# Attention steps of two batches placed at shared moments, and batch 2's landmarks summed on VectorE

## The chip, the cores and the metric

One core of one Trainium2 chip runs the whole kernel in one launch. The metric is the device time of that launch in microseconds (us), lower is better. The engines are named as in the profile: PE is TensorE's matmul stream, PEld its weight loads, DVE is VectorE, ACT ScalarE, POOL GpSimd, and SP is SyncE, whose queue issues most of the DMAs.

## What is computed

Nystrom attention over 8 batches of 8 heads (576 positions, head dimension 64, 32 landmarks), then a mixture of experts in which a token takes an expert of its own or keeps that of the token before it. Cut to what matters:

```python
q_lm = q.reshape(B, H, m, S // m, D).mean(axis=3)      # landmarks: means of 18 rows, m = 32
k_lm = k.reshape(B, H, m, S // m, D).mean(axis=3)
A, Bm, C = sm(q, k_lm), sm(q_lm, k_lm), sm(q_lm, k)    # softmax(scale * a @ b.T)
Z = Bm.transpose(0, 1, 3, 2) / (norm1(Bm) * norminf(Bm) + 1e-06)
for _ in range(6):
    Z = 2 * Z - Z @ Bm @ Z
x = A @ Z @ C @ v
...
fresh_e = int(np.argmax(logits[b, s]))
e = fresh_e if s == 0 or local_gate[b, s] < 0.5 else prev_e
out[b, s] = p[e] * (np.maximum(x[b, s] @ w1[e], 0.0) @ w2[e])
```

All inputs and outputs are float32.

## The kernel before

The tokens of a batch nearly all go to one expert, so the kernel finds that expert, `own` (L500), and runs a dense two-layer product for the batch with it; tokens of other experts are gathered at the end into slots of 128 (`slot_tokens`, `slots_end`). Batches are in a pipeline: while `expert` (L837) runs for one batch, the attention of the next is worked off in between.

**The expert.** For each of 8 batches `expert` goes over 16 steps: two passes (of 320 and of 256 rows) with 8 blocks of the hidden layer each. In a step PE does six products of the first layer (L819, into a `ph` bank), and then those of the second layer for the block before (L861 into `py` banks, L870 into `pg`). Operands are split in a high and a low part (`gh`/`gl`, `ath`/`atl`, `wh`/`wl`, `h`), which makes three products of each. These are PE's large products, on the full 128 x 128 array. For each block ACT and DVE turn the `ph` bank into `h` (L826, L831, for batch 0 also `hx` L828, L834); for each weight block ACT casts (L806) and POOL subtracts (L808).

**The attention of one batch** is a chain of small steps. `landmarks` (L190) sums 18 rows: two POOL additions of 128 x 288 (L200, into the tile `t9`) and a DVE reduction (L202), for each half of q and k. `scores_c` (L239) makes the scores of C and Bm (L251) in two groups; each group takes two of the three banks named `one`, which its exps on ACT (L262, L266) set free. `norms` (L308) is a chain of 13 small DVE instructions (L311 to L336), `newton_product` (L345) and `newton_start` (L349, L350) open the iteration, and six `newton_step` follow (PE L358, ACT L360, DVE L361). `c_transpose` (L278) and `c_v` (L297) give C @ v, `newton_w` (L365, L367), `newton_wt` (L374) and `newton_gate` (L384) give the gate's weights. `scores_a` (L398, L402), `a_max`, `a_exp`, `a_norm`, `a_back` make A. Then `gates` (L447), `fresh`, `sticky` (L481, L483, L485), `chosen` (L491 to L497), `own` (L504 to L511) choose the expert; SP reads its number and `load_w1`/`load_w2` fetch its weights. `own_rest` (L514 to L528, eight DVE instructions) and `a_split` (L434, L436) follow. `w_w1` (L774) folds the gate's weights into the first layer (PE L785, ACT L791, DVE L794).

PE runs the small products with the array cut into tiles: 32 rows by 32 columns for L345, L358, L365; 64 by 32 for L251, L384, L398, L785; 128 by 32 for L447 and most of L297. Only the transposes L278 and L374 and the sum L504 use the full array. In PE's stream a run of small products between two large ones is called a burst here.

**What sets the order.** A clock counts expert steps: batch b of the expert lasts from 16 b to 16 b + 16 (`CH` = 16). A step's `tick` calls move the clock by a quarter and emit every action that is due, `at_time(t, fn, ...)`; a `yield 0.25` inside an action puts its rest a quarter of a step later. Each engine then executes in the order of emission. `attention(b)` (L1090) gives the due times of batch b relative to t0 = (b - 1) * 16:

```python
at_time(t0 - 0.75, scores_c, st, 0)
at_time(t0 + 0.5, scores_c, st, 1)
ta, tn = [t0 + t for t in (-2.75, -1.75, -0.75, 3.25, 4, 5.5)], t0 + 2
...
for k in range(6):
    at_time(tn + 1.5 + 0.5 * k, newton_step, b, st, k)
```

So a batch's attention lies within some 14 steps, its Newton iteration within three. Batch 0's attention is `startup` (L538), ahead of all expert work, written out by hand; batch 1's whole attention lies in batch 0's expert steps, with due times of its own.

Of the kernel before, what the change touches and what calls it, by code (L numbers as in the profile page):

```python
# [23 lines left out]
P = 128  # L24
# [36 lines left out]
def nystrom_attn_then_sticky_moe(ctx, tc, qT, kT, v, wg, w12, out):  # L61
# [152 lines left out]
    def landmark_parts(st, t, a):  # L214
# [5 lines left out]
        def part(n):  # L220
# [18 lines left out]
    def scores_c(st, g, d=0.5):  # L239
# [5 lines left out]
        pc = [one.tile([P, 512]) for _ in range(2)]  # L245
# [268 lines left out]
    def own_rest(b, st):  # L514
# [4 lines left out]
                                in1=others.unsqueeze(2).broadcast_to([P, E, NBLK]), op=ALU.mult)  # L519
        pe = st["pe"]  # L520
# [17 lines left out]
    def startup(st, nx):  # L538
# [550 lines left out]
    CH = 2 * NC2  # L1089
    def attention(b):  # L1090
        st, t0 = sts[b], (b - 1) * CH
        if b > 1:
            at_time(t0 - (13 if b == 2 else 14), load, b, st)
            at_time(t0 - 11, load_v, b, st)
            for t, x, a in ((-10, "k", 0), (-9, "k", 2), (-8, "q", 0), (-7, "q", 2)):
                t = t if b > 2 else 0.75 * t
                at_time(t0 + t, landmarks, b, st, x, a)
            at_time(t0 - 0.75, scores_c, st, 0)
            at_time(t0 + 0.5, scores_c, st, 1)
            ta, tn = [t0 + t for t in (-2.75, -1.75, -0.75, 3.25, 4, 5.5)], t0 + 2  # L1100
# [3 lines left out]
        at_time(ta[0], scores_a, b, st, 0)
        at_time(ta[1], scores_a, b, st, 1)
        at_time(ta[2], a_max, b, st)
        at_time(ta[3], a_exp, st)
        at_time(ta[4], a_norm, b, st)
        at_time(ta[5], a_back, st)
        at_time(tn, norms, b, st)  # L1110
        at_time(tn + 0.5, newton_product, b, st)
        at_time(tn + 1.25, newton_start, b, st)
        for k in range(6):
            at_time(tn + 1.5 + 0.5 * k, newton_step, b, st, k)
        for k, t in enumerate((1, 1.75, 2.25)):
            at_time(tn + t, c_transpose, st, 2 * k)
        at_time(tn + 3.25, c_v, st)
        at_time(tn + 4.5, newton_w, b, st)
        at_time(tn + 5, newton_wt, b, st)
        at_time(tn + 5.5, newton_gate, b, st)  # L1120
        at_time(tn + 6.25, gates, st)
        at_time(tn + 6.5, fresh, st)
        at_time(tn + 7.25, sticky, st)
        at_time(tn + 8.25, chosen, st)
        at_time(tn + 8.75, own, b, st)
        at_time(tn + 9, get_w1, b)
        at_time(tn + 9.25, own_rest, b, st)
        at_time(tn + 9.5, a_split, b, st)
# [16 lines left out]
    at_time(3.5, lambda: w_w1(sts[0], 1))  # L1145
    at_time(7.25, own_rest, 0, sts[0])
# [67 lines left out]
```

## Time and profile before

| | |
|---|---|
| time, median of 3 runs | 523.0 us (520.9 to 524.95) |
| time of the profiled execution | 525.08 us |
| its span, first to last instruction | 523.4 us |
| PE busy | 482.6 us (92%), mean granted clock 0.962 |
| DVE, ACT, POOL busy | 325.2, 210.5, 192.6 us (62, 40, 37%) |
| DMA | 82.58 MB, mean 158 GB/s |

The page's strip of 40 slices of 13 us shows where PE is not busy and where its clock is low:

```profile
PE   6757879888999999999999999999999999889994
PEclk9759997889899999999999999999999999999998
```

A PE matmul's duration contains its passage through the array, and the next one starts before it ends. What a product costs is the distance from its start to the start of the next one. A wait is idle time of an engine, put down to what ended it.

### The profile page before, as it was taken

The page shows a single profiled execution, that of the slowest core. Times are in us where ns is not written, and L with a number is a line of the kernel's source. Part 1 is how long each engine was busy: PE and PEld are TensorE (multiplying, and loading weights), DVE is VectorE, ACT ScalarE, POOL GpSimd, SP SyncE. Part 2 cuts the span into 40 slices and gives each one's busy share as a digit, 9 for nine tenths or more (in the row PEclk, how much of TensorE's full clock was granted, in tenths as well). Part 3 has the DMA queues.
Part 4 walks back from the last instruction along what each step waited for, and adds up shares of the span by engine and source line. Part 5 has one row for each costly group of instructions (what it writes and reads, how often), then busy time and mean ns, then how long its engine had stood idle before and what let it go on. Part 6 is the DMA issues. An engine that isn't in the chain of part 4 may idle for free. (4 is left out here: it accounts for less than half of the span.)

```text
span 523.4 us, 12143 instructions
## 1 busy us (share of the span) xinstructions
PE 482.6 (92%) x4722; PEld 343.2 (66%) x4722; DVE 325.2 (62%) x957; ACT 210.5 (40%) x538; POOL 192.6 (37%) x206
## 2 busy tenths in 40 slices
PE   6757879888999999999999999999999999889994
PEld 2423557645777677757786677767775777668774
DVE  6876663847456764867476756676476736986230
ACT  2425432336224561447243722464144714341361
POOL 5212261343430562244422453166225501240653
PEclk9759997889899999999999999999999999999998
DMA  8448432284126643366317731763345111734340
GB/s 291 170 148 302 194 93 97 80 292 181 59 90 212 227 173 130 108 234 255 141 46 274 277 107 45 270 235 138 101 163 190 62 58 45 287 96 157 100 163 20
DMA packets 38621, 82.58 MB, mean 158 GB/s; under 512 B 3179, under 2 KB 4459, under 8 KB 37792
## 3 DMA queue, kind: packets, MB, share of 16 engines
q1 hardware_dynamic: 37072, 76.71, 41.4%
q0 software_dynamic: 1488, 5.07, 2.6%
q8 instruction: 38, 0.62, 0.5%
q14 instruction: 23, 0.19, 0.1%
HBM read 66.34 MB, written 15.47 MB: 156 GB/s over the span
## 5 line engine op out<-in xcount | busy, mean ns | idle before, releaser
L861 PE MATMUL py<-wh,h 128*128 128x512 f32 x528 | 175.1, 414 | 0.1
L808 POOL TENSOR_TENSOR wl<-raw,wh 128x512 fp32r<-128x512 f32 x72 | 92.0, 1285 | 149.5 <-ACT wh L806 106.9
L861 PEld LDWEIGHTS py<-wh,h 128*128 128x128 f32 x528 | 91.9, 191 | 31.6 <-issue 13.8
L831 DVE SCALAR_TENSOR_TENSOR h<-ph,h 128x256 fp32r<-128x256 f32 (+1 forms) x136 | 55.6, 409 | 86.2 <-ACT h L826 80.5
L826 ACT ACTIVATE h<-ph 128x256 fp32r<-128x256 f32 (+2 forms) x136 | 54.7, 403 | 123.0 <-PE ph L819 115.3
L861 PE MATMUL py<-wl,h 128*128 128x512 f32 x264 | 89.0, 416 | 0.0
L819 PE MATMUL ph<-ath,gh 128*128 128x320 f32 (+1 forms) x256 | 81.4, 318 | 5.6 <-DVE gl L794 1.8
L819 PE MATMUL ph<-ath,gl 128*128 128x320 f32 (+1 forms) x256 | 76.4, 298 | 0.1
L819 PE MATMUL ph<-atl,gh 128*128 128x320 f32 (+1 forms) x256 | 76.2, 298 | 0.0
L819 PEld LDWEIGHTS ph<-ath,gh 128*128 128x128 f32 x256 | 49.0, 191 | 19.7 <-issue 7.5
L861 PEld LDWEIGHTS py<-wl,h 128*128 128x128 f32 x264 | 46.0, 190 | 13.3 <-issue 3.9
L806 ACT CAST wh<-raw 128x512 fp32r<-128x512 f32 x72 | 45.1, 629 | 14.8 <-DMA raw<-w 14.8
L819 PEld LDWEIGHTS ph<-atl,gh 128*128 128x128 f32 x256 | 49.1, 192 | 2.9
L819 PEld LDWEIGHTS ph<-ath,gl 128*128 128x128 f32 x256 | 48.9, 191 | 0.4 <-DVE gl L794 0.4
L200 POOL TENSOR_TENSOR t<-k_t 128x288 f32<-128x288 f32 x24 | 17.4, 748 | 46.0 <-DVE sk L202 45.9
L361 DVE TENSOR_TENSOR et<-et,one 128x64 f32<-128x64 f32 x42 | 9.2, 220 | 35.5 <-ACT et L360 28.4
L899 POOL TENSOR_TENSOR ys<-ys,yl 64x512 f32<-64x512 f32 x8 | 10.4, 1294 | 49.0 <-ACT yl L897 49.0
L200 POOL TENSOR_TENSOR t<-q_t 128x288 f32<-128x288 f32 x24 | 17.3, 744 | 29.6 <-DVE sq L202 15.7
L360 ACT COPY et<-one 128x64 f32<-128x64 f32 x35 | 7.4, 212 | 44.0 <-PE one L358 43.0
L888 ACT ACTIVATE ys<-py,pall 128x512 f32<-128x512 f32 x32 | 20.4, 695 | 10.5 <-PE py L861 8.8
L794 DVE TENSOR_TENSOR gl<-pg,gh 128x512 fp32r<-128x512 f32 (+1 forms) x19 | 12.5, 660 | 19.1 <-ACT gh L791 19.1
L791 ACT CAST gh<-pg 128x512 fp32r<-128x512 f32 (+1 forms) x19 | 10.7, 564 | 32.5 <-PE pg L785 32.5
(313 smaller groups left out, 778.3 us busy)
## 6 DMA issues: line engine op xcount, KB each, us to landing
raw<-w SPq DMA_DIRECT2D x72, 256.0 KB, 5.5
raw<-w SPq DMA_DIRECT2D x17, 1024.0 KB, 7.1
v_t<-v SPq DMA_DIRECT2D x8, 1024.0 KB, 6.2
out<-ys SPq DMA_DIRECT2D x32, 256.0 KB, 2.2
q_t<-qT SPq DMA_DIRECT2D x6, 1152.0 KB, 5.5
k_t<-kT SPq DMA_DIRECT2D x6, 1152.0 KB, 8.2
ad<-sa POOLq DMA_DIRECT2D x8, 576.0 KB, 3.6
q_t<-qT SPq DMA_DIRECT2D x4, 576.0 KB, 9.1
```

The source lines that it names most:

```text
L200: nc.gpsimd.tensor_add(t9[:, i], src[:, a + i, :, 0:9], src[:, a + i, :, 9:18])
L361: nc.vector.tensor_add(new[:, :, 32:64], et[:, :, 32:64], pn[:, :, 32:64])
L791: nc.scalar.copy(out=gh[:, g, x], in_=ps[g])
L794: nc.vector.tensor_tensor(out=gl[:, g, x], in0=ps[g], in1=gh[:, g, x].bitcast(F32), op=ALU.subtract)
L806: nc.scalar.copy(out=wh, in_=raw)
L808: nc.gpsimd.tensor_tensor(out=wl, in0=raw, in1=wh.bitcast(F32), op=ALU.subtract)
L819: mm = nc.tensor.matmul(hp, w[:, g, c], x[:, g, s0:s0 + n], start=(i == 0), stop=(i == 5))
L826: nc.scalar.activation(out=h[:, 0:e], in_=hp[:, 0:e], func=AF.Relu)
L831: nc.vector.scalar_tensor_tensor(out=h[:, 384:384 + m], in0=hp[:, 0:m], scalar=0.0, in1=h[:, 0:m].bitcast(F32), op0=ALU.max, op1=ALU.subtract)
L861: nc.tensor.matmul(yps[k], h[:, part + i * P:part + i * P + P], w, start=(f == 0 and part == 0 and w is wh), stop=(f == NC2 - 1 and part = ...
L888: nc.scalar.mul(out=ys, in_=yp, mul=st["pw"][:, k:k + 1])
L899: nc.gpsimd.tensor_tensor(out=ys[0:64], in0=ys[0:64], in1=yl[0:64], op=ALU.add)
```

## The change

Nothing of the arithmetic changes. What changes is when, and in two places by whom, it is done:

- `attention` takes its due times from three tables: `FIRST` for batch 1, `SECOND` for batch 2, `STEADY` for the others. In `STEADY` the scores of C come 13 steps earlier (-13.75 and -11.75 rather than -0.75 and 0.5), the Newton steps lie 1.5 or 2 steps apart (0.5 before), and loads and landmarks come some 12 steps earlier. Modulo 16 the PE steps of the early part of a batch fall on the same due times as those of the late part of the batch before it, ten in all, with both `w_w1` on two of them.
- Batch 2's landmarks are reduced on DVE straight from q and k (`landmarks_alone`, eight reductions, L225), not added on POOL first.
- Batch 1's second group of C scores takes the two `py` banks.
- `own_rest` of batch 0 moves from step 7.25 into `startup`, and `own_rest` yields half a step in the middle. In `startup` the exps of a C group go ahead of the first `w_w1` on ACT, and one landmark reduction goes behind the start of the expert.
- The first casts of batch 1's second-layer weights (`cast_w2`) come 1.75 steps later, and `w_w1` of later batches a quarter earlier (`G0`).

```diff
+    def landmarks_alone(st, t, a):
+        part = landmark_parts(st, t, a)
+        part(2)
+        yield 0.25
+        s = part(2, False)
+        yield 0.5
+        landmark_scale(st, t, a, s)
...
-        pc = [one.tile([P, 512]) for _ in range(2)]
+        pc = [(bank or one).tile([P, 512]) for _ in range(2)]
...
+        yield 0.5
         pe = st["pe"]
...
+        rest = own_rest(0, st)
+        next(rest)
         next(c0)
         nc.vector.tensor_tensor(out=al, in0=full, in1=ah.bitcast(F32), op=ALU.subtract)
         lk2(2)
         g0 = w_w1(st, 0, 0, 2)
+        at_once(c0)
         next(g0)
-        at_once(c0)
         at_once(g0)
-        lk2(2)
+        at_once(rest)
+        at_time(0.3, lk2, 2)
...
+    STEADY = dict(load=-26, landmarks=(-22.75, -21.5, -20.25, -19), load_v=-14, scores_c=(-13.75, -11.75), norms=-10.75,
+                  product=-10.25, start=-9.5, newton=(-8.75, -7.25, -5.75, -3.75, -2.25, -0.75), turn=(-8.75, -7.25, -5.75),
+                  scores_a=(-3.75, -2.25), a_max=-1.5, a_exp=0.5, a_norm=1.25, a_back=3.25, c_v=-0.75, w=0.75, wt=2.25, gate=4.25,
+                  gates=5.75, fresh=6.25, sticky=7.25, chosen=8.75, own=10.25, w1=10.5, own_rest=11, split=12)
+    SECOND = dict(STEADY, load=-14, landmarks=(-11.25, -10.5, -9.75, -9), load_v=-6, scores_c=(-8.75, -7.25), norms=-6.25,
+                  product=-5.75, start=-5.25, newton=(-4.75, -3.75, -2.25, -0.75, 0.75, 2.25), turn=(-5.75, -4.75, -3.75),
+                  scores_a=(-2.25, -0.75), a_max=0, a_exp=1.5, a_norm=2.25, a_back=4.25, c_v=0.75, w=3.25, wt=4.25, gate=5)
+    FIRST = dict(norms=3, product=3.5, start=4, newton=(4.25, 4.75, 5.25, 5.75, 6.25, 6.75), turn=(4.25, 4.75, 5.25),
+                 scores_a=(2.25, 4.25), a_max=4.75, a_exp=6, a_norm=6.75, a_back=8, c_v=6.25, w=7.25, wt=7.75, gate=8.25,
+                 gates=8.75, fresh=9.25, sticky=10.25, chosen=11, own=11.75, w1=12, own_rest=12.25, split=12.5)
...
-            at_time(1.25, scores_c, st, 1, 0.25)
-            ta, tn = [2.25, 4.25, 5, 6.25, 7, 8.25], 3
...
+            at_time(1.25, scores_c, st, 1, 0.25, Banks((py, "py")))
...
-    G0, G1, W2, C2 = 14, 16.75, 11, 14
+    G0, G1, W2, C2 = 13.75, 16.75, 11, 14
...
-            at_time(t0 + (G0, G1)[hf] + (0.75, 0.5)[hf] * (b == 1), lambda b=b, hf=hf: w_w1(sts[b], hf))
+            at_time(t0 + (G0, G1)[hf] + (b == 1) * (1 - hf), lambda b=b, hf=hf: w_w1(sts[b], hf))
...
-            at_time(t0 + C2 + 0.9 * f, cast_w2, b, f)
+            at_time(t0 + C2 + 1.75 * (b == 1) + 0.9 * f, cast_w2, b, f)
...
-    at_time(3.5, lambda: w_w1(sts[0], 1))
-    at_time(7.25, own_rest, 0, sts[0])
+    at_time(3.45, lambda: w_w1(sts[0], 1))
```

The order on the engines shows it at three places. The changed kernel has other line numbers for the same statements: L358 stands as L367 there, L278 as L287, L481 as L490, L819 as L832, L861 as L874, L870 as L883, L361 as L370, L367 as L376, L517 to L528 as L526 to L538, L256 to L260 as L265 to L269, L753 as L765, L794 as L807, L831 and L834 as L844 and L847, L806 as L819, L826 as L839, L791 as L804.

First PE in a steady batch, before: two Newton steps of one batch, and four transposes of C between them, each alone between large products.

```order
L358 MATMUL one<-et 32x64 x8
L861 MATMUL py<-wl,h 128x512 x2
L278 MATMUL one<-ident,ec_3005 128x128
L278 MATMUL one<-ident,ec_3075 128x128
L278 MATMUL one<-ident,ec_3005 128x128
L278 MATMUL one<-ident,ec_3075 128x128
L861 MATMUL py<-wh,h 128x512 x2
L870 MATMUL pg<-wh,h 128x512
L870 MATMUL pg<-wl,h 128x512
L358 MATMUL one<-et 32x64 x8
```

And in the changed kernel, where `sticky` of one batch, a Newton step of the next and its transposes stand in one burst.

```order
L490 LDWEIGHTS d_2757
L490 MATMUL one<-identb,d_2757 1x64
L367 MATMUL one<-et 32x64 x8
L287 MATMUL one<-ident,ec_2595 128x128
L287 MATMUL one<-ident,ec_2668 128x128
L287 MATMUL one<-ident,ec_2595 128x128
L287 MATMUL one<-ident,ec_2668 128x128
L874 MATMUL py<-wh,h 128x512 x2
```

Three bursts of the order before have become one; over a batch 24 bursts have become ten.

Second DVE in batch 0, before: the last Newton step of batch 1 (L361), all of batch 0's `own_rest`, the `h` of a block, and `newton_w`'s product `wc` (L367), for which PE's transposes L374 wait.

```order
L361 TENSOR_TENSOR et<-et,one 128x2x32
L517 TENSOR_SCALAR others<-desc_81,mxc 128x8
L518 TENSOR_TENSOR oh<-ohb,others 128x8x5
L522 TENSOR_REDUCE psum<-pe 128x5
L523 TENSOR_SCALAR psum<-psum 128x5
L524 RECIPROCAL psum<-psum 128x5
L525 TENSOR_TENSOR pe<-pe,ohb 128x40
L526 TENSOR_REDUCE psum<-pe 128x5
L528 TENSOR_TENSOR pall<-psum 128x5
L831 SCALAR_TENSOR_TENSOR h<-ph,h 128x256
L834 SCALAR_TENSOR_TENSOR hx<-ph,hx 128x64
L367 TENSOR_TENSOR wc<-one,rc 128x256
```

And in the changed kernel at the same place, from the last Newton step of batch 1 (L370) to `wc` (L376) and on. The first `own_rest` now stands ahead of all of batch 0's expert work.

```order
L370 TENSOR_TENSOR et<-et,one 128x2x32
L427 TENSOR_REDUCE rsa<-sa 128x36
L428 TENSOR_SCALAR rsa<-rsa 128x36
L429 RECIPROCAL rsa<-rsa 128x36
L225 TENSOR_REDUCE sq<-q_t 128x32
L376 TENSOR_TENSOR wc<-one,rc 128x256
L225 TENSOR_REDUCE sq<-q_t 128x32
L844 SCALAR_TENSOR_TENSOR h<-ph,h 128x256
L847 SCALAR_TENSOR_TENSOR hx<-ph,hx 128x64
```

In place of the eight instructions of `own_rest`, one of batch 2's eight landmark reductions (L225) stands ahead of `wc`; six more of them lie earlier in the same stretch.

Third ACT at the end of batch 0, before: a cast of batch 1's second-layer weights, which waits for their DMA, ahead of the last blocks of `h` and of `w_w1`'s `gh`.

```order
L806 CAST wh<-raw_1293 128x512
L826 ACTIVATE h<-ph 128x256
L791 CAST gh<-pg 128x512
L791 CAST gh<-ph 128x512
L806 CAST wh<-raw_1326 128x512
L826 ACTIVATE h<-ph 128x256
```

And in the changed kernel, with the first cast behind both.

```order
L839 ACTIVATE h<-ph 128x256
L804 CAST gh<-pg 128x512
L804 CAST gh<-ph 128x512
L210 ACTIVATE ql<-sq 128x64
L839 ACTIVATE h<-ph 128x256
L369 COPY et<-one 128x2x32
L819 CAST wh<-raw_1408 128x512
```

The casts (L806, now L819) have moved behind two blocks of `h` and the `gh` of `w_w1`.

## Rows read from the trace of the kernel before

**Rows 1.** Windows from a batch's first L819 to the next batch's, of batch 0 and of batch 3, which stands for the steady ones. The columns are the stretch in us from the span's start, its length, the busy time (and instructions) of PE, PEld, DVE, ACT and POOL, PE's granted clock as a share of 2.4 GHz, the DMA engines' busy share, and GB/s.

```profile
42.57:115.78 73.21, 61.90 (x604) 42.09 (x605) 45.17 (x128) 26.61 (x76) 26.23 (x23) 0.91 0.46 162
...
231.50:287.49 55.99, 55.87 (x569) 40.22 (x568) 35.67 (x109) 24.59 (x63) 21.50 (x21) 1.00 0.48 173
```

**Rows 2.** Waits of PE over the whole span: the waiting tile and line, the engine, tile and line that ended the wait, us in total, times, the longest.

```profile
PE one L374 <- DVE wc L367: 4.0, 1, 4.0
PE one L358 <- DVE et L350: 2.1, 1, 2.1
PE one L504 <- DVE ohb L497: 2.0, 1, 2.0
...
PE ph L819 <- DVE gl L794: 1.8, 1, 1.8
PE ph L819 <- DVE h L831: 1.7, 1, 1.7
...
PE one L251 <- ACT ec L266: 1.7, 3, 0.7
PE one L398 <- ACT ec L266: 1.3, 1, 1.3
...
PE one L345 <- DVE s L324: 1.1, 1, 1.1
```

**Rows 3.** Windows of the four stretches after startup in which PE's clock is half (columns as in rows 1).

```profile
76.92:83.75 6.83, 4.65 (x30) 3.68 (x31) 4.03 (x11) 0.76 (x2) 1.83 (x3) 0.50 0.28 107
97.40:100.82 3.42, 3.29 (x12) 2.90 (x13) 2.94 (x10) 0.72 (x2) 1.94 (x3) 0.50 0.00 0
111.06:114.47 3.41, 3.41 (x23) 1.59 (x22) 3.41 (x7) 1.48 (x4) 2.03 (x3) 0.50 0.38 106
131.54:134.95 3.41, 3.41 (x26) 2.40 (x25) 1.74 (x3) 0.21 (x2) 1.46 (x1) 0.50 0.02 5
```

**Rows 4.** Timeline of PE around one Newton step of a steady batch: start, duration (passage included), line, operation, tiles, array tile, shape, count.

```profile
245.86 0.40 PE L870 MATMUL pg<-wh,h 128*128 128x512 f32 x1
246.10 0.40 PE L870 MATMUL pg<-wl,h 128*128 128x512 f32 x1
246.42 0.43 PE L358 MATMUL one<-et 32*32 32x64 f32 x16
246.78 0.41 PE L819 MATMUL ph<-ath,gh 128*128 128x320 f32 x1
247.03 0.31 PE L819 MATMUL ph<-atl,gh 128*128 128x320 f32 x1
247.18 0.31 PE L819 MATMUL ph<-ath,gl 128*128 128x320 f32 x1
```

**Rows 5.** The same view of the same burst, cut off at 246.50 and then at 246.61: what of it had begun by then.

```profile
246.42 0.26 PE L358 MATMUL one<-et 32*32 32x64 f32 x4
...
246.42 0.37 PE L358 MATMUL one<-et 32*32 32x64 f32 x12
```

**Rows 6.** The same view of two cuts through `c_v` (L297), which needs products of 128 and of 64 rows: 252.3 to 252.4, which shows the run of 128 rows that it meets from its group at 252.09 on, and 252.57 to 252.735, which shows the run of 64 rows from its start.

```profile
252.09 0.46 PE L297 MATMUL one<-v_t,ect 128*32 128x64 f32 x20
...
252.49 0.49 PE L297 MATMUL one<-v_t,ect 64*32 64x64 f32 x9
```

**Rows 7.** The same view of four full-array transposes between large products.

```profile
241.02 0.74 PE L861 MATMUL py<-wh,h 128*128 128x512 f32 x2
241.60 0.63 PE L861 MATMUL py<-wl,h 128*128 128x512 f32 x2
242.07 0.60 PE L278 MATMUL one<-ident,ec 128*128 128x128 f32 x4
242.42 0.71 PE L861 MATMUL py<-wh,h 128*128 128x512 f32 x2
242.97 0.39 PE L870 MATMUL pg<-wh,h 128*128 128x512 f32 x1
```

**Rows 8.** Timeline of POOL and DVE from 73.4 to 78.9 us, in batch 0; in brackets the idle time ahead of an instruction and what ended it.

```profile
73.51 2.13 POOL L422 TENSOR_TENSOR sa<-sa,rsa 128x1152 f32<-128x1152 f32 x1 [2.00 <-DVE et L361]
73.61 2.08 DVE L518 TENSOR_TENSOR oh<-ohb,others 128x40 bf16<-128x40 bf16 x1
...
77.86 0.39 DVE L528 TENSOR_TENSOR pall<-psum 128x5 f32<-128x5 f32 x1
...
78.64 0.41 DVE L367 TENSOR_TENSOR wc<-one,rc 128x256 f32<-128x256 f32 x1
```

**Rows 9.** The same view of the first and last instruction of the next `own_rest`, batch 1's.

```profile
100.33 0.21 DVE L517 TENSOR_SCALAR others<-desc,mxc 128x8 f32<-128x8 f32 x1
...
101.66 0.17 DVE L528 TENSOR_TENSOR pall<-psum 128x5 f32<-128x5 f32 x1
```

**Rows 10.** Groups by line on DVE in the first 60 us: tiles, count, busy us, mean ns of one, idle time ahead.

```profile
L225 DVE TENSOR_REDUCE sk<-k_t 128x32 f32<-128x576 f32 x4 | 3.0, 741 | 0.0
```

**Rows 11.** The longest wait of ACT in batch 0's stretch (columns as in rows 2).

```profile
ACT wh L806 <- DMA raw<-w: 6.3, 1, 6.3
```

**Rows 12.** Timeline of POOL: the first instruction after the stretch in which `own_rest` of batch 0 lies in the changed kernel, with POOL's idle time ahead of it.

```profile
46.05 1.27 POOL L808 TENSOR_TENSOR wl<-raw,wh 128x512 fp32r<-128x512 f32 x1 [16.51 <-ACT wh L806]
```

**Rows 13.** Timeline of DVE: the first instruction of batch 1's `norms` and the last of its `newton_start`.

```profile
53.63 0.16 DVE L311 TENSOR_SCALAR rsb<-sb 128x2 f32<-128x2 f32 x1
...
59.01 0.23 DVE L350 TENSOR_TENSOR et<-et,id 128x64 f32<-128x64 f32 x1
```

More of the change, by code (lines that the diff above doesn't have):

```diff
@@ L218, in landmark_parts, with part @@
         s, done = sm.tile([P, 2, M], F32, name="s" + t), [0]
-        def part(n):
+        def part(n, scale=True):
             i, r = a + done[0] // 2, slice(16 * (done[0] % 2), 16 * (done[0] % 2) + 16 * n)
@@ L226, in part @@
             done[0] += n
-            if done[0] == 4:
+            if done[0] == 4 and scale:
                 landmark_scale(st, t, a, s)
+            return s
         return part
+    def landmarks_alone(st, t, a):
[5 more added lines that the diff above has]
+        landmark_scale(st, t, a, s)
     def each_head(fn):
@@ L237, in each_head, with scores_c @@
                 fn(g, c, slice(64 * (h % 2), 64 * (h % 2) + 64), h // 2)
-    def scores_c(st, g, d=0.5):
+    def scores_c(st, g, d=0.5, bank=None):
         if g == 0:
@@ L1090, in attention @@
     def attention(b):
         st, t0 = sts[b], (b - 1) * CH
-        if b > 1:
[L1093 to L1100, printed above, removed]
-        else:
-            at_time(1.25, scores_c, st, 1, 0.25)
-            ta, tn = [2.25, 4.25, 5, 6.25, 7, 8.25], 3
@@ L1104, in attention @@
[L1104 to L1128, printed above, removed]
-    G0, G1, W2, C2 = 14, 16.75, 11, 14
+        t = {1: FIRST, 2: SECOND}.get(b, STEADY)
@@ new lines, in steps, with step @@
+        def steps(name, fn, *args):
+            for i, x in enumerate(t[name]):
+                at_time(t0 + x, fn, *args, i)
+        def step(name, fn, *args):
+            at_time(t0 + t[name], fn, *args)
+        if b > 1:
+            step("load", load, b, st)
+            step("load_v", load_v, b, st)
+            for x, (y, a) in zip(t["landmarks"], (("k", 0), ("q", 0), ("k", 2), ("q", 2))):
+                if b == 2:
+                    at_time(t0 + x, landmarks_alone, st, y, a)
+                else:
+                    at_time(t0 + x, landmarks, b, st, y, a)
+            steps("scores_c", scores_c, st)
+        else:
+            at_time(1.25, scores_c, st, 1, 0.25, Banks((py, "py")))
@@ new lines, in attention @@
+        step("norms", norms, b, st)
+        step("product", newton_product, b, st)
+        step("start", newton_start, b, st)
+        steps("newton", newton_step, b, st)
+        steps("turn", lambda i: c_transpose(st, 2 * i))
+        steps("scores_a", scores_a, b, st)
+        step("c_v", c_v, st)
+        step("a_max", a_max, b, st)
+        step("a_exp", a_exp, st)
+        step("a_norm", a_norm, b, st)
+        step("a_back", a_back, st)
+        step("w", newton_w, b, st)
+        step("wt", newton_wt, b, st)
@@ L1131, in nystrom_attn_then_sticky_moe @@
+        step("gate", newton_gate, b, st)
+        step("gates", gates, st)
+        step("fresh", fresh, st)
+        step("sticky", sticky, st)
+        step("chosen", chosen, st)
+        step("own", own, b, st)
+        step("w1", get_w1, b)
+        step("own_rest", own_rest, b, st)
+        step("split", a_split, b, st)
+    G0, G1, W2, C2 = 13.75, 16.75, 11, 14
     for b in range(1, B):
```

## The prediction

> **What bounds the kernel now.** I read the windows by batch first. In a steady batch PE is busy for 55.87 of 55.99 us at full clock, while DVE has 35.67 and ACT 24.59: there PE's own stream is the bound, and only less or cheaper work on PE shortens it [rows 1]. Batch 0 takes 73.21 us with almost the same number of products; PE is busy for only 61.90 of them and the granted clock is 0.91, so some 11 us of it are waits and some are slow clock [rows 1]. The list of PE's waits says which: 4.0 us for `wc`, 2.0 for `ohb`, 1.7 for `h`, 1.3 for `ec` and 1.1 for `s` lie in batch 0, 2.1 for `et` in batch 1, 1.7 in three batches together for `ec`, and 1.8 for `gl` ahead of the slots [rows 2]. Behind the waits of 1.7 us and more stand four stretches at a granted clock of 0.50, that is at 1.2 rather than 2.4 GHz; PE was busy in them for 4.65, 3.29, 3.41 and 3.41 us [rows 3]. Work that takes 14.76 us at half clock takes 7.4 at the full one, so the low clock costs 7.4 us. The waits of 1.1 and 1.3 us in batch 0 left no such stretch.
>
> **What a burst costs.** The timeline shows the price around one Newton step [rows 4]. A product of 512 columns is followed by its like after 0.24 us (245.86, 246.10), but by the first small one after 0.32: 0.08 more. The sixteen small ones stand in four groups of four. After the first four, eight more begin within 0.11 us [rows 5], and a group follows a group each 0.056 us (my working from these starts), so sixteen take 0.22 us; the burst occupies 0.36, 0.14 more. The first large product after it is followed after 0.25 us, where its like is after 0.15: 0.10 more. In and out of the tiled array cost 0.08 + 0.14 + 0.10, with the starts unrounded 0.33 us, which is more than the work inside. Changing the rows inside a burst is cheaper: `c_v`'s twenty products from 252.09 are five groups, so the next is due at 252.37, and the first one of 64 rows starts at 252.49 [rows 6]; with 0.02 us for its slower first group I take 0.14. Full-array transposes are free of it: behind four of them two L861 take 0.55 us to the next product, where the same pair took 0.58 ahead of them (241.02 to 241.60) [rows 7].
>
> **The merging.** Counted in the order of the two kernels behind startup: 178 bursts become 92. Of those that go from the full array into tiles there were 136 and are 83, 53 fewer, 53 x 0.33 = 17.6 us. Against that, changes of the row size inside a burst rise from 1 to 44, 43 x 0.14 = 5.9. Net **-11.7 us**, some 1.7 in each steady batch and less in the first two. The Trainium skill ("TensorEngine Tiling (Array Packing)", section "Tiling Modes", key properties) says that changing the tiling mode, not just the tile, drains TensorE. By that a change of rows is a drain too, and my trace agrees as far as 0.14 us is not nothing; what it would be as a full drain is a rival below.
>
> **Batch 0's waits.** `wc` comes late because `own_rest` stands ahead of it on DVE (shown in the order) while POOL runs L422: L518 takes 2.08 us and ends when POOL does, and from L518 to the end of L528 it is 4.6 us [rows 8], where batch 1's whole `own_rest` takes 1.5 [rows 9]. The Trainium skill ("SBUF — State Buffer", section "Who interferes with whom") says that a DVE instruction with two SBUF inputs and a GpSimd instruction that reads SBUF exclude each other, and that a reduction never does so on trn2. The trace agrees: L225's reductions take 741 ns [rows 10]. Moved into startup, `own_rest` meets a POOL that is idle for 16.51 us [rows 12], so there it costs DVE 1.5 us, in a stretch in which POOL's next work is far off; I take nothing on the path, and at most its 1.5 us if DVE is what PE awaits there. The 4.0 us goes, and so does the 2.0 for `ohb`, whose DVE queue was the same. The 1.7 for `h` stands behind an ACT that sits 6.3 us in a cast waiting for its DMA [rows 11]; with the casts behind two blocks of `h` (shown in the order) that wait holds only casts. The 1.3 for `ec` goes, since the group takes banks of its own, and the 1.1 for `s` since `norms` begins earlier against its product. Together **-10.1 us**.
>
> **Other waits.** The 2.1 in batch 1 goes with batch 2's Newton iteration spread out; the 1.7 for `ec` at L251 because C's scores now come 13 steps earlier, with the exps done before the banks are wanted; the 1.8 for `gl` because `w_w1` comes a quarter earlier: **-5.6 us**. With the waits goes the half clock behind them, **-7.4 us**.
>
> **What comes in their place.** Batch 2's landmarks add eight reductions of 0.74 us, 5.9 us, to DVE in batch 0 [rows 10]; six lie ahead of `wc`. `own_rest` leaves, and more of batch 2's chain moves in: 45.17 us of DVE becomes an estimated 52 of some 61. One reduction that starts just ahead of a due instruction delays it by up to 0.74 us, two by 1.5. So I enter two waits of 1.1 us in batch 0 behind that backlog, and 1.0 in batch 1. The first step of batch 1's Newton iteration is due soon after `norms`: from L311 to the end of L350 it is 5.6 us on DVE [rows 13], and PE has some 3.5 us of large products to do meanwhile (some 15 at the distances of [rows 4]), short by 2.1; the bursts and the products of `norms`' own steps lie between too, so I enter 1.4. For the `py` banks, now also taken by C's scores, 0.4. Sum **+5.0 us**, between 0 (each hidden) and 11 (the 4.0 and 2.0 as they are now, and 5.0). The steady steps show no chain that gets shorter than it is: between two Newton steps lie 1.5 steps of the expert or more, 5.2 us by the window of batch 3 [rows 1], against 0.5 before. Loads of q and k are asked for 12 steps earlier and no transfer is later than its user; in batch 3 the DMA engines are at 0.48 [rows 1], so I take nothing, and up to 2 us if a weight block comes behind them.
>
> **Sum.** The profiled execution took 525.1 us: 525.1 - 11.7 - 10.1 - 5.6 - 7.4 + 5.0 = 495.3. It lies 2.1 above the median of 523.0, so on the median's scale 493.
>
> **Rivals.**
> - *The new waits don't occur* (all of the 5.0 is hidden): 488. For it: DVE still has 9 us to spare in batch 0. Against it: the reductions stand just ahead of `wc`.
> - *DVE becomes the bound of batch 0.* The eight reductions and two-input operations held by POOL bring back waits of 4.0 and 2.0 us, with the half clock behind them (4 us, as in the stretch at 76.92 with the next one): +10, 503. For it: DVE is at 52 of 61 us and its order is dense where POOL runs L422 [rows 8].
> - *A change of rows inside a burst is a full in-and-out*: 43 x 0.33 = 14.2 rather than 5.9, +8.3, 501. For it: the rule on modes above, which makes no difference between the two. Against it: the row of `c_v` at 0.14 [rows 6], though there the columns stay and only the rows change.
> - *The change doesn't merge what it seems to*: bursts on the same due time get separated by waits for semaphores, and only half the merging arrives: +6, 499. Against it: the order of the changed kernel shows them side by side, and a wait would have to fall in nearly every one.
> - *Slower.* The merged bursts hold PE's large products back in one piece, and all ACT and DVE work of a moment falls due at once, so that `h` of the next block comes late at each of 10 moments in 7 batches. From the 30 us that the change gains, it decides at 30/70 = 0.43 us a moment; at 0.6 it is +42, 535. Against it: a moment has some 5 us of large products behind it in which ACT and DVE are idle for a third and more of the time [rows 1].
>
> **How the numbers follow.** The forecast of 493 gets 0.52, hidden waits 0.13, DVE as the bound 0.18, full drains 0.08, half the merging 0.03, slower 0.04, and something unnamed that leaves the time within 1% 0.02. For the range I go from 486 (hidden waits and 2 us for odds) to 508 (DVE as the bound, with the upper end of its waits); outside it lie the slower rival, drains together with DVE, and a mis-sized gain in waits. A measurement of this kernel can tell about 1% from no change, 5.2 us: the first five cases, 0.94, are faster by far more. So 0.94 faster, 0.02 same, 0.04 slower.
>
> **What would show it.** In a steady batch's window: some 54.3 us in place of 56, PE still busy throughout at clock 1.0. In the timeline around a merged burst: one entry of 0.08 and one exit, with 0.14 at each change of rows. In the waits: no `wc`, `ohb`, `h`, `ec` above 1 us, no granted clock of 0.5 after the start of the expert, batch 0 in some 61 us. If steady batches stay at 56, the burst price is wrong; if batch 0 stays above 66, DVE's backlog is.

## The result, and the profile after

The changed kernel takes 493.2 us (median of 4 runs, 492.8 to 493.7) against 522.9 in the same comparison: a ratio of 0.9433, 95% interval 0.9395 to 0.9470. The forecast was 493. Its profiled execution took 493.74 us, its span is 491.9.

The page's strip of the changed kernel, 40 slices of 12.3 us:

```profile
PE   6758999999999999999999999999999999899994
PEclk9858999999999999999999999999999999999999
```

Behind slice 4 no slice of the clock is below 9, and PE is below 9 in one slice only until the slots. The windows by batch of the changed kernel, first batch 0, then batch 3, then batch 6 (columns as in rows 1):

```profile
41.36:103.81 62.45, 59.96 (x709) 41.61 (x710) 51.10 (x158) 29.66 (x92) 23.13 (x21) 1.00 0.60 213
...
215.51:269.60 54.09, 53.45 (x568) 41.06 (x567) 37.51 (x110) 24.87 (x63) 22.03 (x21) 1.00 0.53 180
...
376.68:425.11 48.43, 45.27 (x305) 35.59 (x303) 25.57 (x82) 18.95 (x38) 15.35 (x17) 1.00 0.37 132
```

Against [rows 1] batch 0 is 10.8 us shorter although it now holds 105 more products (709, 604 before), at a clock of 1.00 rather than 0.91; DVE has 51.1 us of work in it. Batch 3 is 1.9 us shorter with the same products. It is no longer without gaps: PE is idle for 0.64 us in it. Batch 6 no longer holds the early steps of batch 7, which now lie a batch earlier, and there is no batch 8 whose early steps could take their place; PE is idle for 3.2 us in it. The waits of PE over the span, those that are new or changed (the others stood before too):

```profile
PE ph L832 <- DVE gl L807: 4.2, 7, 0.7
...
PE one L367 <- DVE et L359: 1.5, 2, 0.8
...
PE ph L832 <- DVE h L844: 1.0, 1, 1.0
PE ph L798 <- DVE h L844: 1.0, 1, 1.0
...
PE ph L832 <- DVE h L847: 0.5, 1, 0.5
...
PE one L456 <- ACT ec L275: 0.3, 1, 0.3
```

Of [rows 2], the waits for `wc`, `ohb` and `s`, that for `h` in batch 0, those of L251 and L398 (now L260 and L407) for `ec`, and the one of 2.1 us for `et` at the old place are gone. Of the 1.8 us for `gl` ahead of the slots 0.7 are left, at the end of batch 6. New are 0.6 us for `gl` in each of batches 0 to 4 and 0.3 in batch 7, 0.8 for `et` in batches 0 and 1, and `h` in batch 6.

The timeline of PE around the merged burst that the order above shows (start, duration, line, tiles):

```profile
240.05 0.31 PE L832 MATMUL ph<-ath,gl 128*128 128x320 f32 x1
240.29 0.50 PE L490 MATMUL one<-identb,d 128*1 128x128 bf16 x5
240.72 0.43 PE L367 MATMUL one<-et 32*32 32x64 f32 x16
241.08 0.66 PE L287 MATMUL one<-ident,ec 128*128 128x128 f32 x4
241.49 0.72 PE L874 MATMUL py<-wh,h 128*128 128x512 f32 x2
242.05 0.63 PE L874 MATMUL py<-wl,h 128*128 128x512 f32 x2
```

One entry (0.24 us behind a product of 320 columns, where the like takes 0.15), no large product between the three pieces, and one exit. The sixteen L367 occupy 0.36 us until the transposes, as they did alone [rows 4], so their own exit is not saved; what is saved is each piece's entry and the slower first large product behind it.

### The profile page after: what moved, and what is told of

Same layout as the page of the kernel before. It is cut to its first block, busy times and chain, and to the rows that moved or that the text cites. A ratio compares the mean times of both kernels' runs of the same rounds, so it can differ in the third digit from the quotient of the medians.

```text
span 491.9 us, 12153 instructions
## 1 busy us (share of the span) xinstructions
PE 461.4 (94%) x4722; PEld 342.2 (70%) x4722; DVE 326.4 (66%) x961; ACT 211.2 (43%) x538; POOL 186.9 (38%) x198
## 4 chain that ended last, share of the span: by engine, by line
PE 66%; DVE 23%; issue 3%; ACT 3%; DMA 2%; POOL 2%; SPq 0%; POOLq 0%; ACTq 0%; DVEq 0%
PE py L874 27%; PE ph L832 16%; PE pg L883 5%; PE one L260 3%; PE one L306 2%; PE one L367 2%; DVE gl L807 2%; DVE h L844 2%; PE one L287 2%; PE ph L798 2%; DVE psum L533 2%; DMA k_t<-kT 1%; DVE sa L411 1%; DVE sq L202 1%; DVE sk L202 1%
## 5 line engine op out<-in xcount | busy, mean ns | idle before, releaser
L874 PE MATMUL py<-wh,h 128*128 128x512 f32 x528 | 171.8, 407 | 0.1
L839 ACT ACTIVATE h<-ph 128x256 fp32r<-128x256 f32 (+2 forms) x136 | 54.5, 400 | 177.0 <-PE ph L832 159.8
L874 PEld LDWEIGHTS py<-wh,h 128*128 128x128 f32 x528 | 89.5, 188 | 31.4 <-issue 20.2
L844 DVE SCALAR_TENSOR_TENSOR h<-ph,h 128x256 fp32r<-128x256 f32 (+1 forms) x136 | 54.9, 407 | 66.6 <-ACT h L839 64.5
L832 PE MATMUL ph<-ath,gh 128*128 128x320 f32 (+1 forms) x256 | 77.7, 304 | 6.9 <-DVE gl L807 3.5
L874 PE MATMUL py<-wl,h 128*128 128x512 f32 x264 | 83.4, 395 | 0.0
L832 PE MATMUL ph<-ath,gl 128*128 128x320 f32 (+1 forms) x256 | 75.8, 296 | 0.6 <-DVE gl L807 0.6
L832 PE MATMUL ph<-atl,gh 128*128 128x320 f32 (+1 forms) x256 | 75.5, 295 | 0.0
L832 PEld LDWEIGHTS ph<-ath,gh 128*128 128x128 f32 x256 | 48.2, 188 | 19.1 <-issue 5.7
L874 PEld LDWEIGHTS py<-wl,h 128*128 128x128 f32 x264 | 49.2, 188 | 10.8
L832 PEld LDWEIGHTS ph<-atl,gh 128*128 128x128 f32 x256 | 48.3, 189 | 4.2
L832 PEld LDWEIGHTS ph<-ath,gl 128*128 128x128 f32 x256 | 48.2, 188 | 1.2 <-DVE gl L807 1.0
L200 POOL TENSOR_TENSOR t<-q_t 128x288 f32<-128x288 f32 x20 | 14.5, 748 | 87.4 <-DVE sk L202 87.4
L819 ACT CAST wh<-raw 128x512 fp32r<-128x512 f32 x72 | 44.2, 618 | 0.0
L431 POOL TENSOR_TENSOR sa<-sa,rsa 128x1152 f32<-128x1152 f32 x7 | 14.9, 2132 | 18.9 <-PE one L383 14.3
L883 PE MATMUL pg<-wh,h 128*128 128x512 f32 x56 | 21.9, 392 | 0.0
L883 PE MATMUL pg<-wl,h 128*128 128x512 f32 x56 | 21.9, 392 | 0.0
L807 DVE TENSOR_TENSOR gl<-pg,gh 128x512 fp32r<-128x512 f32 (+1 forms) x19 | 12.4, 652 | 11.8 <-ACT gh L804 11.8
L419 POOL TENSOR_TENSOR sa<-sa,mxa 128x1152 f32<-128x1152 f32 x7 | 14.9, 2132 | 11.4 <-DVE mxa L417 10.7
```

The source lines that it names most:

```text
L419: nc.gpsimd.tensor_tensor(out=sa, in0=sa, in1=mx.unsqueeze(2).broadcast_to([P, 2 * NJ, M]), op=ALU.subtract)
L431: nc.gpsimd.tensor_tensor(out=sa, in0=sa, in1=rs.unsqueeze(2).broadcast_to([P, 2 * NJ, M]), op=ALU.mult)
L807: nc.vector.tensor_tensor(out=gl[:, g, x], in0=ps[g], in1=gh[:, g, x].bitcast(F32), op=ALU.subtract)
L819: nc.scalar.copy(out=wh, in_=raw)
L832: mm = nc.tensor.matmul(hp, w[:, g, c], x[:, g, s0:s0 + n], start=(i == 0), stop=(i == 5))
L839: nc.scalar.activation(out=h[:, 0:e], in_=hp[:, 0:e], func=AF.Relu)
```

## The experiments

All are edits of the changed kernel unless it says otherwise. The ratios are to the kernel before, measured beside each; the differences given are those of the medians to the changed kernel's 493.2 us. Taken by the ratios, they come out up to 0.9 us larger or smaller.

**Merging undone.** The early steps of batches 3 to 7 half a step earlier.

```diff
-    STEADY = dict(... scores_c=(-13.75, -11.75), norms=-10.75, product=-10.25, start=-9.5,
-                  newton=(-8.75, -7.25, -5.75, -3.75, -2.25, -0.75), turn=(-8.75, -7.25, -5.75),
+    STEADY = dict(... scores_c=(-14.25, -12.25), norms=-11.25, product=-10.75, start=-10,
+                  newton=(-9.25, -7.75, -6.25, -4.25, -2.75, -1.25), turn=(-9, -7.5, -6),
```

> The changed kernel with the early PE steps of batches 3 to 7 half a step earlier (the transposes of C a quarter), so that they share no moment with the batch before: 152 bursts in place of 92, 35 more entries into the tiled array and 31 fewer changes of rows inside a burst. Theory (a burst's passage in and out costs 0.33 us, an inner change 0.14): 35 x 0.33 - 31 x 0.14 = +7.2 us, 500. Rival (the steady batches gain from early C scores, not from merging): no change, 493.

It took 501.5 us, ratio 0.9591 (0.9554 to 0.9628): +8.3. Batch 4 in its windows:

```profile
274.04:329.50 55.46, 55.14 (x568) 40.59 (x567) 38.45 (x110) 24.74 (x63) 21.91 (x21) 1.00 0.52 175
```

PE is busy for 55.14 us with the products that take 53.45 in the changed kernel's batch 3, so it is the merging, and not the earlier scores, that shortens PE's own stream: 1.7 us a batch come back with 60 of the 86 bursts. Over all windows behind startup PE is busy for 8.4 us more, with the same 4341 products, and idle for 1.0 less.

**`own_rest` put back.** It stands at step 7.25 of batch 0 again.

```diff
-        rest = own_rest(0, st)
-        next(rest)
...
-        at_once(rest)
...
+    at_time(7.25, own_rest, 0, sts[0])
```

> The changed kernel with own_rest of batch 0 back at step 7.25. Theory (own_rest behind POOL was what made wc late, and the half clock followed that wait): a wait of 2 to 4 us returns in batch 0 with up to 3.4 us of half clock, 497 to 501. Rival (DVE has room in batch 0 now that wc lies elsewhere): under 1 us, 493 to 494.

499.3 us, ratio 0.9535 (0.9499 to 0.9571): +6.1. Its timeline of POOL, DVE and PE in batch 0:

```profile
70.94 2.13 POOL L431 TENSOR_TENSOR sa<-sa,rsa 128x1152 f32<-128x1152 f32 x1 [3.16 <-DVE rsa L429]
...
71.65 1.45 DVE L526 TENSOR_SCALAR others<-desc,mxc 128x8 f32<-128x8 f32 x1
73.03 1.28 POOL L818 TENSOR_TENSOR wl<-raw,wh 128x512 fp32r<-128x512 f32 x1
73.13 1.24 DVE L527 TENSOR_TENSOR oh<-ohb,others 128x40 bf16<-128x40 bf16 x1
...
79.14 1.28 PE L456 MATMUL one<-at,wgc 128*32 128x160 f32 x16 [3.59 <-DVE wgc L396]
```

L526 takes 1.45 us where it takes 0.21 undisturbed [rows 9], and ends as POOL's L431 ends; L527 ends as L818 ends. PE then waits 3.59 us, now for `wgc`, which stands behind both halves of `own_rest` in DVE's queue. Behind the wait its clock is half for 6.83 us:

```profile
77.18:84.01 6.83, 4.87 (x37) 2.59 (x38) 4.29 (x18) 1.08 (x5) 0.00 (x0) 0.50 0.58 209
```

The stretch begins inside the wait. 3.6 us of wait and 4.87/2 = 2.4 of clock are 6.0; batch 0 is 5.7 us longer (68.10).

**`own_rest` alone moved**, in the kernel before.

```diff
+        yield from ()
...
+        at_once(own_rest(0, st))
         next(c0)
         nc.vector.tensor_tensor(out=al, in0=full, in1=ah.bitcast(F32), op=ALU.subtract)
...
-    at_time(7.25, own_rest, 0, sts[0])
```

> The kernel before with only own_rest of batch 0 moved into startup. Theory: the wait of 4.0 us for wc and the half clock behind it (4.65 us of PE work at half speed, 2.3 us) go: -6.3, 517. Rival (wc is late by batch 0's whole chain, not by own_rest): less than -2 us, 521 or more.

518.3 us against 523.2, ratio 0.9892 (0.9858 to 0.9927): -4.9, short of the 6.3 that were expected. The wait for `wc` and the half clock behind it are gone, and batch 0 takes 69.02 us rather than 73.21, although a new stretch of half clock stands at 45.58 us (see the last section). But the wait of 2.0 us for `ohb` stays, so that one was not `own_rest`'s:

```profile
PE one L504 <- DVE ohb L497: 2.0, 1, 2.0
PE ph L821 <- DVE h L833: 1.5, 1, 1.5
PE one L398 <- ACT ec L266: 1.3, 1, 1.3
PE one L345 <- DVE s L324: 1.1, 1, 1.1
```

**Casts at their old times.**

```diff
-            at_time(t0 + C2 + 1.75 * (b == 1) + 0.9 * f, cast_w2, b, f)
+            at_time(t0 + C2 + 0.9 * f, cast_w2, b, f)
```

> The changed kernel with the first casts of batch 1's second-layer weights at their old due times, 1.75 steps earlier. Theory (ACT waits in the cast for the DMA, h comes late, and the clock falls behind that wait): 1.7 us of wait and up to 3.4 of PE work at half clock return, 495 to 497. Rival (batch 0 is shorter now but the weights come at the same distance from their issue, and ACT waits without holding PE): no change, 493.

499.3 us, ratio 0.9551 (0.9524 to 0.9578): +6.1, more than expected. In batch 0 PE waits once for 2.3 us, at 104.56, and the clock is half from 104.30 to 107.71; in the same batch ACT waits in the cast:

```profile
ACT wh L819 <- DMA raw<-w: 5.3, 1, 5.3
```

Batch 0 takes 66.55 us, 4.1 more than in the changed kernel: 2.3 of wait, 1.6 of clock. That is the theory's mechanism at its size. The other 2 us are in startup (+1.4) and in batch 7 (+1.9), less 0.8 in batch 1; the edit touches none of these three (see below).

**C scores of batch 1 in the banks `one`.**

```diff
-            at_time(1.25, scores_c, st, 1, 0.25, Banks((py, "py")))
+            at_time(1.25, scores_c, st, 1, 0.25)
```

> The changed kernel with batch 1's second group of C scores in the banks named one again, rather than the two py banks. Theory (the wait of 1.3 us for ec was for a bank that the exps of C hold): a wait of about 1.3 us returns in batch 0, 494.5. Rival (the spread of the due times is enough): no change, 493.

496.5 us, ratio 0.9511 (0.9473 to 0.9550): +3.3. In batch 0 one wait is back, of the expected size, and the batch is 64.02 us long, 1.6 more:

```profile
PE one L407 <- ACT ec L275: 1.3, 1, 1.3
```

The rest is again startup (+0.7) and batch 7 (+1.9), less 1.0 in batches 1 and 4.

**Batch 2's landmarks added on POOL first.**

```diff
-                    at_time(t0 + x, landmarks_alone, st, y, a)
+                    at_time(t0 + x - 1.75, landmarks, b, st, y, a)
```

> The changed kernel with batch 2's landmarks added on POOL first, as in other batches (each 1.75 steps earlier, so that they are done in time). DVE loses 3 us of work in batch 0, POOL gets 6. Theory (the eight reductions put DVE's queue back by about a microsecond in places, and POOL's additions hold two-input operations of DVE instead): within 2 us of 493. Rival (DVE's work bounds batch 0): under 491. Second rival (POOL's holds bound it): over 496.

501.6 us, ratio 0.9601 (0.9575 to 0.9628): +8.4, far outside what I expected; the number is the second rival's. The profiled execution is 6.0 us above the changed kernel's: 4.2 in batch 0, 1.9 in batch 7, 0.8 in startup, less 0.9 elsewhere. DVE has 3.3 us less to do in batch 0 (47.8), POOL 5.6 more (28.7), and the batch takes 66.68 us, 4.2 more. The place in its timeline:

```profile
65.85 1.45 POOL L200 TENSOR_TENSOR t<-q_t 128x288 f32<-128x288 f32 x2
67.26 2.13 POOL L419 TENSOR_TENSOR sa<-sa,mxa 128x1152 f32<-128x1152 f32 x1
69.35 1.27 POOL L821 TENSOR_TENSOR wl<-raw,wh 128x512 fp32r<-128x512 f32 x1
69.42 1.16 ACT L422 ACTIVATE sa<-sa 128x1152 f32<-128x1152 f32 x1 [4.35 <-POOL sa L419]
...
71.11 0.22 DVE L370 TENSOR_TENSOR et<-et,one 128x64 f32<-128x64 f32 x1 [5.55 <-ACT et L369]
...
71.38 0.33 PE L367 MATMUL one<-et 32*32 32x32 f32 x16 [1.97 <-DVE et L370]
```

POOL's additions stand ahead of its L419, ACT's exp L422 waits 4.35 us for L419, the Newton step's copies stand behind that exp on ACT, and PE waits 1.97 us for them, with 3.41 us of half clock behind it (72.74 to 76.15). So the second rival's mechanism, POOL holding DVE, isn't what this chain shows, but POOL being late for ACT: what DVE took over was POOL's time on a chain. How much of it the earlier due times of this run add was not tried apart.

**The new wait for `gl`.** The timeline of the changed kernel shows what stands ahead on DVE:

```profile
262.49 0.75 DVE L202 TENSOR_REDUCE sq<-t 128x64 f32<-128x576 f32 x1 [0.93 <-POOL t L200]
...
263.16 0.84 DVE L411 STREAM_TRANSPOSE sa<-one 128x288 f32<-128x288 f32 x2
...
263.92 0.65 DVE L807 TENSOR_TENSOR gl<-pg,gh 128x512 fp32r<-128x512 f32 x1
...
264.49 0.68 DVE L807 TENSOR_TENSOR gl<-ph,gh 128x512 fp32r<-128x512 f32 x1
...
265.32 0.35 PE L832 MATMUL ph<-ath,gh 128*128 128x256 f32 x1 [0.64 <-DVE gl L807]
```

The casts of `gh` were done at 263.12; `gl` begins 0.8 us later, behind a landmark's reduction and two transposes, and PE waits 0.64 us for the `ph` bank. Moving the landmark by half a step:

```diff
-    STEADY = dict(load=-26, landmarks=(-22.75, -21.5, -20.25, -19), ...
+    STEADY = dict(load=-26, landmarks=(-22.75, -21.5, -20.25, -18.5), ...
```

> The changed kernel with the fourth landmark of batches 3 to 7 half a step later, so that its reduction on DVE stands behind the gl of w_w1 rather than ahead of it. Theory (PE's new wait of 0.6 us a batch for gl is that reduction, 0.75 us, ahead on DVE's queue): the wait goes in five batches, -3 us, 490. Rival (the wait is for the ph bank by the two stream transposes ahead of gl, the reduction only fills a hole): under -1 us, 492 to 493.

490.3 us, ratio 0.9364 (0.9335 to 0.9394): -2.9. The wait goes in four batches, 1 to 4; the one of batch 0 stands at another place, 54.8 us, and stays at 0.60. The steady batch is gapless again, 53.27 us, all of it PE:

```profile
213.83:267.10 53.27, 53.27 (x568) 41.13 (x567) 37.05 (x109) 25.01 (x63) 22.05 (x21) 1.00 0.53 183
```

**Three edits together**, the landmark, the chain of the slots three steps later, and `c_v`'s second group with its block of 64 rows first:

```diff
-            c_v_rows(st, pv, g, range(NBLK))
+            c_v_rows(st, pv, g, (0, 1, 2, 3, 4) if g == 0 else (4, 0, 1, 2, 3))
...
-                                 ..., start=(k == 0), stop=(k == NBLK - 1))
+                                 ..., start=(k == (4 if blocks[0] == 4 else 0)), stop=(k == (3 if blocks[0] == 4 else NBLK - 1)))
...
-    at_time((B - 2) * CH + 12, others)
-    at_time((B - 1) * CH + 2.5, slot_tokens, sts[B])
-    at_time((B - 1) * CH + 5, slots_end)
+    at_time((B - 2) * CH + 15, others)
+    at_time((B - 1) * CH + 4.5, slot_tokens, sts[B])
+    at_time((B - 1) * CH + 6.5, slots_end)
```

> The changed kernel with three edits: the fourth landmark half a step later as in the run before; the chain of DVE instructions that sorts the slots (others) 3 steps later, and what follows it 2 and 1.5, out of the steps in which batch 7's last attention steps fill DVE; and in c_v the second group takes its 64-row block first, which saves one change of rows a batch. Theory: -2.9 for the landmark, -2.5 for the waits for h and gl in batch 6, 7 x 0.14 = -1.0 for the change of rows: 487. Rival (the waits of batch 6 move into batch 7, and a change of rows costs a full 0.33 us): 490 - 2.3 = 488, with waits for h or gl in batch 7.

491.5 us, ratio 0.9408 (0.9385 to 0.9431): no gain over the landmark alone. Its windows of batches 3, 6 and 7:

```profile
213.27:266.38 53.11, 53.11 (x568) 41.11 (x567) 37.21 (x110) 24.98 (x63) 22.12 (x21) 1.00 0.53 183
372.32:417.53 45.21, 44.74 (x305) 35.76 (x304) 20.80 (x66) 18.89 (x38) 14.28 (x14) 1.00 0.37 130
417.53:465.78 48.25, 44.16 (x283) 34.39 (x282) 31.82 (x83) 16.36 (x34) 19.41 (x20) 1.00 0.32 105
```

The steady batch is 0.16 us shorter, the price of one change of rows. Batch 6 is 3.1 us shorter (45.21, 48.31 with the landmark alone), and batch 7 is 3.1 longer (48.25, 45.20). Part of this is waits that moved with the chain, as the rival said: in batch 7 PE now waits 1.12 and 0.85 us for `h` where the other kernel has no such wait. The late signals told at the end of the next section lie in this batch 7 too, so how much moved isn't shown.

**Landmark and `c_v` only**, and **the same with POOL's constants early**: the two memsets of `segs` (L920, L921) at `slots_begin`. DVE's waits in batch 6 of the changed kernel had shown why:

```profile
DVE inc L927 <- POOL segs L921: 4.2, 1, 4.2
```

```diff
     def slots_begin():
...
+        segs = xs["segs"] = xp.tile([P, E * B, NBLK], F32, name="segs")
+        nc.gpsimd.memset(segs, 1.0)
+        nc.gpsimd.memset(segs[:, :, 0:1], 0.0)
```

> The changed kernel with the fourth landmark half a step later and the second group of c_v taking its 64-row block first, the slots' chain where the change has it. Theory: -2.9 for the wait for gl and 7 x 0.14 = -1.0 for a change of rows less in each batch, 489.3, a steady batch 0.13 to 0.14 shorter than with the landmark alone. Rival (a change of rows is a full passage in and out): 7 x 0.33 = -2.3, 488.

> The same with one more edit: POOL sets the tile segs to its constants when the slots' memory is opened, six steps earlier, rather than behind POOL's addition for a store. Theory (DVE stands still for 4.2 us in batch 6 for that tile, and the waits of PE for h and gl behind it are the backlog): the 2.7 us of waits in batch 6 go without coming back in batch 7, 486.6. Rival (DVE's own work of those steps is the backlog, as moving the chain showed): no change, 489.

They took 492.5 us (ratio 0.9403, 0.9366 to 0.9440) and 491.3 (0.9394, 0.9357 to 0.9431), each above its forecast and its rival. Both steady batches are 53.1 us: 0.14 less than with the landmark alone, so a change of rows costs 0.14, not 0.33. Batch 6 falls from 48.31 to 47.34 us with the constants early. But in both profiles batch 7 is 48.2 and 48.3 us, 3 more than with the landmark alone, whose batch 7 has the same order as the first of the two.

**Is that batch 7 the kernel's or the run's?**

> The same kernel as with the fourth landmark alone, on the chip of this call. In five kernels the profile of batch 7 is 2 to 3 us longer than in the others, with ACT standing 5 us before a first-layer block that is ready, also where batch 7's order is the same. If that belongs to a kernel, this one has none again: 490. If it belongs to a run or a chip, some executions here are at 492 to 493.

> The fourth landmark later and the constants of segs set early, c_v as in the changed kernel. Batch 6 takes some 1 us less than with the landmark alone (47.3 against 48.3), as it did with c_v reordered: 489 where batch 7 is short, 491 where it is long. Rival (the waits of batch 6 come back in batch 7): 490.

The same kernel as with the landmark alone took 491.1 us here (single times 489.9 to 492.3; 489.5 to 490.4 the first time), ratio 0.9388 (0.9358 to 0.9419): its executions spread over 2.5 us without any edit. Its profile showed the short batch 7 (45.19), so the long one has not been seen in this kernel, only a spread of the size. With the constants of `segs` early and nothing else the time was 489.4, ratio 0.9358 (0.9328 to 0.9387), the lowest median of all kernels here and 1.7 us under that of the landmark alone measured beside it: batch 6 takes 46.34 us rather than 48.32, and batch 7 45.29 rather than 45.19:

```profile
214.49:267.72 53.23, 53.23 (x568) 41.14 (x567) 37.35 (x109) 25.02 (x63) 22.01 (x21) 1.00 0.53 183
373.94:420.28 46.34, 45.24 (x305) 35.29 (x303) 25.66 (x81) 18.99 (x38) 15.59 (x17) 1.00 0.37 132
420.28:465.57 45.29, 43.44 (x282) 34.71 (x283) 26.30 (x68) 16.79 (x35) 19.48 (x18) 1.00 0.38 125
```

DVE's wait for `segs` is gone, and its L927 (now L925) waits 0.6 us for PE. So 2 us of the waits in batch 6 were DVE standing still for POOL's constants, and they don't come back.

## Why the prediction was right

The time was forecast within 0.2 us, and that closeness is luck. The new waits were entered 3.5 us too small; merging 1.7 too small, and two gains that were not entered at all, 2.3 us of smaller waits and 1.2 in startup, made up for them. The sum of the profiled execution, 495.3, was met by 493.7.

- **Merging: mechanism right, size too small.** Forecast 1.7 us a steady batch, measured 2.6. Summed over batch 3 of both traces, from the starts, against what a large product takes to its like inside a run: 24 entries become 10 (-1.1 us), 24 slower first large products behind a burst become 10 (-1.4), and the small products themselves take 0.1 less, since the passages out of the tiles that are saved and the changes of rows that are new nearly cancel. That is -2.6; 0.64 of the new wait and 0.1 elsewhere come back, which leaves the 1.9 of the windows. With the landmark moved, the same batch is 2.7 us shorter than before (53.27 us). So the window of 54.09 came near the forecast 54.3 only with a wait in it. The step that failed is "full-array transposes are free of it". I compared the pair behind the transposes (0.55 us) with the pair ahead of them (241.02 to 241.60, 0.58), but that one stands itself behind a burst, of L345. The undisturbed pair is the next one, 241.60 to 242.07, 0.47 [rows 7]: transposes cost 0.09 at the exit, and 5 of the 24 bursts entered free (three of L278, those of L374 and L504), which is 0.4 of the 0.9 that is missing. How the rest splits isn't shown. Nor is a change of rows much cheaper than a passage into the tiles or out of them: the 0.33 is for both, on average 0.17 each, against 0.14. Merging pays because two passages become one change. The Trainium skill ("TensorEngine Tiling (Array Packing)", section "Tiling Modes") has every change of tiling mode drain TensorE; the runs agree in that a change of rows costs 0.14 us and a passage between full array and tiles 0.17 on average.
- **Batch 0's waits and the clock: right in sum, one cause wrong.** The named waits went, and the half clock with them: -10.1 and -7.4. `own_rest` back brings +6.1, the casts back bring 4 in batch 0, the banks back 1.3, each with the wait that was named, though at `wgc` rather than `wc`. Wrong was "and so does the 2.0 for `ohb`, whose DVE queue was the same": it stays when `own_rest` alone moves. Which of the other edits removes it was not tried. The rule in the Trainium skill ("SBUF — State Buffer", section "Who interferes with whom"), that a DVE instruction with two SBUF inputs and a GpSimd instruction that reads SBUF exclude each other, agrees with L527 ending as POOL's L818 ends, 74.37 and 74.31 us. That a reduction is not held, [rows 10] could not show, since POOL stood still then; the changed kernel does: seven of these reductions run beside a POOL instruction and take 0.70 to 0.75 us, five run alone and take 0.73 to 0.75.
- **New waits: too small, and at other places.** Forecast 5.0 us, measured 8.5: `gl` 4.2, `h` 2.5, `et` 1.5, `ec` 0.3. Of those that I entered, the two of 1.1 behind the reductions in batch 0 are one of 0.8 (`et` at batch 2's first Newton step) and 0.3 at L456, the 1.0 of batch 1 is 0.8, the 1.4 at batch 1's first Newton step doesn't occur, and the 0.4 for the `py` banks is 0.1. Of the `gl` waits 0.7 us is what is left of the 1.8 that was to go. What I excluded, "the steady steps show no chain that gets shorter than it is", was wrong: I looked at PE's chains, not at what stands ahead of `gl` in DVE's order at that moment, and a landmark reduction does.
- **Landmarks on DVE** were entered as a cost only. Against the run on POOL they are a gain of 4.2 us in batch 0, since POOL is on a chain there; that run's earlier due times are in this number.
- **Startup** was entered at nothing; it is 1.2 us shorter. In kernels here whose startup is the same it lies between 40.8 and 42.8 us, with 13.7 to 20.5 us of half clock, so the 1.2 us can't be put down to the change.
- From one profiled span to the other it is -31.5 us. Summed over the windows by batch, that is startup -1.2, PE's idle time behind startup -9.5 (26.8 to 17.3), the half clock -7.4, and PE's busy time, reckoned at full clock, -13.4 (446.6 to 433.2, with 4341 products in both). So merging brought 13.4 us against the 11.7 forecast; the waits named above make -15.7 and +8.5, and the other -2.3 are small ones that I didn't name, 1.0 of them for `xa` in the slots and 0.5 at L911. The prices as printed, 53 x 0.33 and 43 x 0.14, make 17.5 and 6.0, not 17.6 and 5.9; the difference is rounding.

Of the rivals none held. DVE is at 51.1 of 62.45 us in batch 0 (52 of 61 forecast) and is not its bound; the slower rival would have needed 0.43 us of wait at each of 70 moments, and the wait for `gl` is 0.3 to 0.7 at 7.

Open is batch 7. In five of the kernels its profile is 1.9 to 3.1 us longer, and each has this piece (here the kernel with landmark, `c_v` and constants):

```profile
459.65 0.66 ACT L839 ACTIVATE h<-ph 128x256 fp32r<-128x256 f32 x2 [5.27 <-PE py L874]
```

ACT stands for 5.27 us and then does two `ph` banks at once, of which PE had finished the first at 455.67 and the second at 457.76. The semaphore events of the traces show that PE's signal came late. In this stretch the updates of PE's semaphore are recorded 2.2 to 2.9 us apart, though PE ends a product that sends one every 0.9 to 1.4 us; in all five profiles ACT starts 0.02 to 0.03 us behind the next update (here 459.62), 3.9 to 4.0 us after the bank was done, while in the eight profiles without the lateness an update follows its product's end by some 0.02 us there. Why the signals are late stays open. All six profiles taken on two of the chips (14 and 7) have them, that of the kernel with three edits too, and none of the six taken on two others (12 and 6), so the lateness goes with the chip or the session and no edit is shown to cause it. It also lies in the times of the undone edits, so those of the casts and the banks are given by batch 0 above, and times of kernels from different sessions differ by it.

## What to carry to other kernels

Where PE is busy without gaps, count what it pays to change between the full and the tiled array: here 0.33 us in and out for a burst, more than the 0.22 of work in a Newton step, and 0.14 for a change of rows inside one, so independent small products belong side by side. Take the undisturbed price of a product from a place with its like on both sides, not from its neighbour. After such a move read every other engine's order at the moments that were filled: here a reduction of 0.75 us ahead of a 0.7 us subtraction cost 3 us over four batches, and half a step gave it back.

## What was not expected of the hardware

A change from 32-row tiles into full-array transposes costs the small products as much as one into large products (0.36 us for sixteen L367 in both cases). The length of a wait alone doesn't tell whether the clock falls. In [rows 2, 3] I had read that the waits of 1.7 us and more have a stretch at half clock behind them, but that is so of four of the five: the 1.8 for `gl` left none. Over all kernels here the waits of 1.97 us and more each have a stretch at half clock that begins within them or behind them, 3.41 us long or, with 3.6 and 4.0 us of wait, 6.83. Of the waits of 1.75 to 1.86 us near the slots those in two kernels have one and those in three have none, and in the kernel before with `own_rest` moved one of 1.52 us has one. There the clock also fell at 45.58 us, behind waits of 0.55 and 0.58 and during one of 0.89, which end at 42.19, 43.47 and 45.81 us; that cost the run some 1.6 of the 6.3 us that were expected of it.
